# First rows of cumulated logarithms: scanned in the operand's partitions instead of sent there

## The chip, the cores and the metric

One core of a Trainium2 chip runs the whole program. The metric is the device time of one execution in microseconds (us). The engines are PE (TensorE, matrix products), DVE (VectorE), ACT (ScalarE) and POOL (GpSimd); SP is the queue from which all DMAs are issued. PEld is PE's weight load.

## What is computed

Causal attention with a decay from forget gates, and behind it two feed-forward layers on its output:

```python
scores = scale * q @ k.T                       # batch 4, heads 8, sequence 576, head size 64
log_f  = np.log(np.clip(f, 1e-4, 1.0))         # f: one gate per (batch, head, position)
cum    = np.cumsum(log_f, axis=-1)
scores = np.where(causal, -1e9, scores + cum[:, :, :, None] - cum[:, :, None, :])
attn   = softmax(scores) @ v
x = relu(x @ w_in) ** 2 @ w_out                # 2304 tokens, 512 -> 2048 -> 512
x = g(x @ w2_in) @ w2_out                      # g: 0 below -1, (h + 1)**2 / 4, h above 1
```

## The kernel before

**Attention of the first 256 positions** runs in groups of four heads of one batch. A group's operand, the tile `QK` (two buffers, used in turn), holds for each head 256 columns of k and 256 columns of q: rows 0 to 63 are the head's data, and the rows below carry the decay, since a product over 128 rows adds `cum` as two more rows. K's row 64 is `cum` against a q row of -8, and q's row 65 is `cum` against a k row of 8; the rows not used are 8 in k and 0 in q. These fills are memsets at the kernel's start (`clear`, L555). So a group needs its data (L605), its v (L626) and its two rows of `cum` (L618, out of `cumd`, a copy of `cum` in DRAM). Its scores come from L643; L589 on DVE takes the mask and the maximum, L650 on ACT the exponential and its sum, L657 and L658 the reciprocal, L673 to L675 scale on ACT, DVE or POOL, L682 transposes on PE, L570/L573 copy to SBUF, and L695 multiplies with v. In names, s0q, E0q, tr0q, av0q belong to group 0, s1q to group 1, and so on. Groups 0 to 3 make the first block of 512 tokens; group 4 and on belong to the second.

**The start.** `setup` loads the gates f of all 32 (batch, head) pairs into 32 partitions (L485), clips them on DVE (L488), takes the logarithm on ACT (L490) and cumulates it with one scan on DVE (L491). The result goes to DRAM (`cumd`, L503), and for group 0 the two rows of each of its four heads go by two DMAs from `cum` straight into `QK` (`first_rows`, L507). Meanwhile PE multiplies the identity with itself 17 times into a bank that nobody reads (`warm_up`, L542). Q2 and K2, tiles of the second kind of attention (positions 256 on), are filled at the start as well (L517, L518).

**Feed-forward.** The first layer's products (L1042) of step s need the weights `whl` of that step; L1093 to L1095 are the second layer's. Weights arrive as 64-bit words (`raw`, L935, 1 MB a step, the first two steps 512 KB), are decoded on ACT, DVE and POOL (L963 to L984), split into a high and a low half (L1016 to L1019), and stored for later blocks in DRAM (`scr`, L1024). The names whl-2 and whl-1 are the two steps ahead of the plain whl. The first block runs through 32 such steps with new weights; later blocks load them back.

**What sets the order.** The whole program is planned: every operation is put down with its alternatives (which engine, at which assumed cost), a due time and what it depends on; `Schedule.improve` places them on five queues with several weightings (`WEIGHTS`) and emits the best plan found. `QE`, `VE` and `RE` give the earliest time at which the first loads of QK, v and raw may be issued. Each engine runs its queue in order, and SP too: a DMA whose data isn't there holds all DMAs behind it.

Of the kernel before, what the change touches and what calls it, by code (L numbers as in the profile page):

```python
# [16 lines left out]
AF = mybir.ActivationFunctionType  # L17
# [5 lines left out]
P = 128  # L23
# [23 lines left out]
OFF = 512  # L47
QUAD = 4
SPARE = ("E", "g", "E", "o", "E", "r", "E", "g", "E", "o")

SLAV = [0.0, 0.51, 0.75, 0.75, 0.0]
SLQK = [0.0, 0.271, 0.412, 0.414, 0.0]
QE = [0.0, 5.4, 8.66, 11.6]
VE = [5.5, 6.1]
RE = [1.36, 7.73, 16.0]
LW = 29.1
WARM = 17

# [63 lines left out]

WEIGHTS = [{}, *({"DVE": x, "POOL": x * y} for x in (0.4, 0.6, 0.8) for y in (0.0, 0.5, 1.0))]

# [256 lines left out]
def tile_attention_moe_moe(ctx: ExitStack, tc: tile.TileContext, qkv, f, w2, outT):  # L381
# [94 lines left out]
    def setup():  # L476
        sb = new("x", "setup", [P, 2 * NKC * 512], F32)
        fr, lf, cum = (lambda i=i: sb.tile[:H * B, S * i:S * i + S] for i in range(3))
        onesf = lambda: sb.tile[:H * B, 3 * S:4 * S]
        due = -100.0  # L480
        G, V_, A = nc.gpsimd, nc.vector, nc.scalar
        tiny_op.append(sch.op(due - 9, {"POOL": (0.05, lambda: G.memset(tiny, 2.0 ** -30))}))
        oh = sch.op(due - 200, {"POOL": (0.05, lambda: G.memset(warm, 0.5))})
        oh = sch.op(due - 200, {"ACT": (1.5, lambda: A.activation(warm, warm, AF.Ln))}, [oh])
        o1 = sch.op(due, {"SP": (dma_t(73728), lambda: nc.sync.dma_start(out=fr(), in_=f))}, bufs=[sb], early=0.0)  # L485
        o2 = sch.op(due - 5, {"POOL": (0.55, lambda: G.memset(onesf(), 1.0))}, bufs=[sb])
        sch.op(due + 90, {"POOL": (0.05, lambda: G.memset(half, 0.5))})
# [4 lines left out]
            cum(), onesf(), lf(), 0.0, op0=ALU.mult, op1=ALU.add))}, [o4, o2], [sb])  # L492
        sch.op(due, {"ACT": (1.4, lambda: A.activation(warm, warm, AF.Exp))}, [o4])
        hi = lambda: fr().bitcast(F32R)
# [9 lines left out]
            out=cumd, in_=cum()[:, :HEAD]))}, [o5], [sb])  # L504

        def first_rows(row, out, due, deps):
            return sch.op(due, {"SP": (dma_t(4096), lambda: nc.sync.dma_start(  # L507
                out=out(), in_=cum()[row:row + QUAD, :HEAD]))}, [o5, *deps], [sb, QK[0]], early=0.0)

        zs = {}  # L510
        due = -30.0
        for i in range(2):
# [9 lines left out]
        for a, z, md in ((OFF + P - HEAD, OFF + P, -100), (0, OFF + P - HEAD, 60)):  # L522
# [7 lines left out]
            fill=1.0, base=0, channel_multiplier=1))}, [i1])  # L530
        return o7, zs, ms, i2, o8, first_rows

    cum_op, zs, mask_op, id_op, cumd_op, first_rows = setup()
    xb = {0: new("x", "x0")}

# [12 lines left out]
    def clear(i, half):  # L548

        n = QUAD * HEAD  # L550
        rows = lambda a, z: QK[i].tile[a:z, n * half:n * half + n]
        kq = lambda a, z, t: rows(a, z).rearrange("p (c t n) -> p c t n", t=2, n=HEAD)[:, :, t, :]
        due = -98 + 2 * i + half
        eng, m = ("POOL", nc.gpsimd) if i else ("DVE", nc.vector)
        fill = lambda out, x: {eng: (n / 1920 + 0.03, lambda: m.memset(out(), x))}  # L555
        kr = sch.op(due, fill(lambda: kq(D, P, 0), 8.0), [], [QK[i]])
        qr = sch.op(due, fill(lambda: kq(D, P, 1), 0.0), [], [QK[i]])
        return [kr, sch.op(due, fill(lambda: kq(D, D + 1, 1), -8.0), [qr], [QK[i]])]
# [34 lines left out]
    def attention32(g):  # L593
# [13 lines left out]
        row = g.b * H + g.h  # L607
        place = lambda t, c0, c1: reg()[D + t:D + t + 1].rearrange("p (c t n) -> p c t n", t=2, n=HEAD)[:, c0:c1, t, :]
        ready = []
        for i in range(parts):  # L610
            c0, c1 = QUAD * i // parts, QUAD * (i + 1) // parts
            if parts == 2:
                if i == 0:
                    rows = [first_rows(row, lambda t=t: place(t, 0, QUAD), -90, [*cleared[0, 0], *cleared[0, 1]])
                            for t in range(2)]
                ready += [[loads[i], *rows]] * (c1 - c0)
            else:
# [607 lines left out]
```

## Time and profile before

| | us |
|---|---|
| median of 3 runs (lowest, highest) | 947.32 (946.98, 948.59) |
| the profiled execution: its time | 946.77 |
| its span, first to last instruction | 945.0 |
| PE, DVE, ACT, POOL busy in that span | 933.9, 585.9, 638.2, 183.3 |
| PE busy in the first 50 us | 43.79 |

The profile is of one execution; 1.8 us of its time lie outside its span. A timeline row gives start, duration, engine, line, operation, output and inputs, shape and count, and in brackets the engine's idle time before it and what ended that. A row that merges several instructions (x4) has the stretch that they cover. A row of the stages view gives length and busy time of each engine in a stretch, with the number of instructions in brackets, the granted clock of PE (1.00 is the upper level, 2.4 GHz), the share of the DMA engines' time and what they moved. The chain of waits follows the program back from its last instruction.

### The profile page before, as it was taken

To read this page: it belongs to the slowest core of one execution; us is meant where nothing else is said; L and a number is where in the kernel's file an instruction comes from. 1 tells how busy PE (TensorE), PEld (TensorE's weight loads), DVE (VectorE), ACT (ScalarE), POOL (GpSimd) and SP (SyncE) were. 2 spreads that over 40 slices of the span, in tenths; PEclk is the share of its full clock that TensorE was granted. 3 is DMA by queue.
4 is the path that set the end of the run, shared out by engine and by line. 5 is a ranking of instruction groups with operands and counts; after the bars stand their busy time and mean duration, and the time that the engine had idled before them with its cause. 6 is when DMAs were issued, how large, how long until landed. Compare 5 with 4: busy or idle time off the path is not lost.

```text
span 945.0 us, 14242 instructions
## 1 busy us (share of the span) xinstructions
PE 933.9 (99%) x4770; PEld 782.9 (83%) x4770; DVE 585.9 (62%) x1319; ACT 638.2 (68%) x1269; POOL 183.3 (19%) x323
## 2 busy tenths in 40 slices
PE   7999999999999999999999999999999999999998
PEld 5677778877888888888788887888888888889998
DVE  8899999899777659776777668775211132220032
ACT  7988889998887868776777677876523343334444
POOL 3300101324231322432223322321000000002200
PEclk9999999999999999999999999999999999999999
DMA  7799998997999997878789887986655555559993
GB/s 217 230 372 367 333 400 307 369 353 262 342 291 294 276 262 214 278 246 267 228 275 295 224 250 224 291 254 188 250 197 196 204 181 203 195 197 373 366 370 143
DMA packets 126105, 254.72 MB, mean 270 GB/s; under 512 B 89808, under 2 KB 90480, under 8 KB 104080
## 3 DMA queue, kind: packets, MB, share of 16 engines
q1 hardware_dynamic: 126032, 253.81, 80.7%
q8 instruction: 38, 0.62, 0.3%
q14 instruction: 35, 0.29, 0.1%
HBM read 194.35 MB, written 38.45 MB: 246 GB/s over the span
## 4 chain that ended last, share of the span: by engine, by line
PE 92%; DVE 3%; DMA 2%; ACT 1%; issue 1%; POOL 0%; SPq 0%; DVEq 0%; ACTq 0%; POOLq 0%
PE h L1042 40%; PE acc L1093 13%; PE acc L1095 13%; PE acc L1094 13%; PE av L866 4%; PE s L787 2%; PE s L788 2%; DMA PT<-PP 1%; DMA raw-2_209<-in_w_dram 1%; DMA out_dram<-o 1%; DVE PP L841 0%; PE s1q L643 0%; PE s7q L643 0%; PE s4q L643 0%; PE s5q L643 0%
## 5 line engine op out<-in xcount | busy, mean ns | idle before, releaser
L1042 PE MATMUL h<-x,whl 128*128 128x512 f32 (+1 forms) x1896 | 434.7, 372 | 0.4 <-DVE whl L1019 0.3
L1042 PEld LDWEIGHTS h<-x,whl 128*128 128x128 f32 x1896 | 325.0, 188 | 56.4 <-issue 3.0
L1093 PE MATMUL acc<-gh,whl 128*128 128x512 f32 (+1 forms) x640 | 239.2, 374 | 0.7 <-ACT o L570 0.7
L1095 PE MATMUL acc<-gl,whl 128*128 128x512 f32 (+1 forms) x640 | 236.8, 370 | 0.0
L1094 PE MATMUL acc<-gh,whl 128*128 128x512 f32 (+1 forms) x640 | 236.3, 369 | 0.0
L582 DVE TENSOR_TENSOR gl<-g,gh 128x512 fp32r<-128x512 f32 (+1 forms) x122 | 82.7, 678 | 123.3 <-PE acc L1095 82.7
L1095 PEld LDWEIGHTS acc<-gl,whl 128*128 128x128 f32 x640 | 120.5, 188 | 21.2 <-POOL gl L584 0.2
L1093 PEld LDWEIGHTS acc<-gh,whl 128*128 128x128 f32 x640 | 120.6, 188 | 18.8 <-ACT o L570 1.3
L1094 PEld LDWEIGHTS acc<-gh,whl 128*128 128x128 f32 x640 | 120.6, 188 | 15.6
L584 POOL TENSOR_TENSOR gl<-g,gh 128x512 fp32r<-128x512 f32 (+1 forms) x38 | 44.4, 1168 | 341.2 <-PE acc L1095 253.1
L1060 ACT ACTIVATE r<-h 128x512 f32<-128x512 f32 (+1 forms) x80 | 43.9, 549 | 86.8 <-PE h L1042 82.9
L1073 DVE SCALAR_TENSOR_TENSOR g<-r,h 128x512 f32<-128x512 f32 (+1 forms) x80 | 50.5, 631 | 80.5 <-ACT r L1071 80.2
L1069 ACT ACTIVATE r<-h,half 128x512 f32<-128x512 f32 (+1 forms) x80 | 51.1, 639 | 61.0 <-PE h L1042 60.5
L841 DVE SCALAR_TENSOR_TENSOR PP<-E,st,PP 128x512 f16<-128x512 f32 (+2 forms) x128 | 78.2, 645 | 10.4 <-ACT PP L837 9.3
L804 ACT ACTIVATE E<-E,st 64x320 f32<-64x320 f32 (+2 forms) x96 | 63.6, 662 | 26.2 <-DVE st L589 15.8
L589 DVE CUSTOM_DVE_ANT_0 E<-s,mask 128x288 f32<-128x288 f32 (+2 forms) x128 | 61.8, 500 | 24.2 <-PE s L788 15.8
L837 ACT ACTIVATE PP<-E,st 128x512 f16<-128x512 f32 (+2 forms) x128 | 68.6, 591 | 6.3 <-DVE st L811 5.7
L866 PEld LDWEIGHTS av<-pr,vt 128*128 128x128 f32 x288 | 53.5, 188 | 12.0 <-ACT r L1069 0.9
L866 PE MATMUL av<-pr,vt 128*128 128x320 f32 (+2 forms) x288 | 61.5, 285 | 0.5 <-DVE st L589 0.5
L570 ACT ACTIVATE gh<-g 128x512 fp32r<-128x512 f32 (+1 forms) x66 | 38.1, 577 | 30.7 <-DVE g L1073 30.4
L575 POOL TENSOR_SCALAR pr<-PT 128x640 fp32r<-128x640 f16 (+2 forms) x49 | 28.5, 583 | 125.9 <-PE av L866 91.1
L1071 ACT ACTIVATE r<-r 128x512 f32<-128x512 f32 (+1 forms) x80 | 46.9, 587 | 2.0
(250 smaller groups left out, 1112.0 us busy)
## 6 DMA issues: line engine op xcount, KB each, us to landing
whl<-scr SPq DMA_DIRECT2D x112, 1024.0 KB
raw<-in_w_dram SPq DMA_DIRECT2D x28, 1024.0 KB
scr<-whl SPq DMA_DIRECT2D x28, 1024.0 KB
in<-in_qkv_dram SPq DMA_DIRECT2D x32, 608.0 KB
whl<-scr SPq DMA_DIRECT2D x32, 512.0 KB
out_dram<-o SPq DMA_DIRECT2D x16, 256.0 KB
QK<-in_qkv_dram SPq DMA_DIRECT2D x7, 512.0 KB
raw<-in_w_dram SPq DMA_DIRECT2D x6, 512.0 KB
```

What stands on the lines that cost most here:

```text
L582: alts["DVE"] = (dve_t(n), lambda: nc.vector.tensor_sub(out(), a(), b()), True)
L589: return nc.vector.tensor_tensor_reduce(out=out, in0=ps, in1=mask[:m, OFF - q0:OFF - q0 + n], scale=scale, scalar=3e38, op0=ALU.add, op1=A ...
L804: nc.scalar.activation(Ec.tile[:m, :e], Ec.tile[:m, :e], AF.Exp, scale=-1.0, bias=nmx(), accum_out=st.tile[:m, 1, ci:ci + 1])))}, [*tops, ...
L837: nc.scalar.activation(hi, x, AF.Copy, scale=r())
L841: nc.vector.scalar_tensor_tensor(lo, x, r(), hi, op0=ALU.mult, op1=ALU.subtract)
L866: nc.tensor.matmul(av.tile[:, c0:W], vt.tile[:, kc, :, :], pr.tile[:, i, :n], start=(kc == 0 and i == 0), stop=(kc == NK - 1))
L1042: nc.tensor.matmul(ps.tile[:, :n], w.tile[:, 0, wi, kc * P:(kc + 1) * P], src.tile[:, kc, xi, :n], start=(kc == 0 and i == 0), stop=(kc == ...
L1069: o1 = sch.op(due, {"ACT": (act_t(n, True, 1), lambda: A.activation(r.tile[:, :n], ps(), AF.Relu, scale=0.5, bias=half))}, [o], [psb, r])
L1073: o2 = sch.op(due, {"DVE": (dve_t(n), lambda: v.scalar_tensor_tensor(g.tile[:, :n], r.tile[:, :n], 1.0, ps(), op0=ALU.min, op1=ALU.max))}, ...
L1093: nc.tensor.matmul(a.tile[:, :n], wh, gh.tile[:, :n], start=(fc == 0), stop=False)
L1094: nc.tensor.matmul(a.tile[:, :n], wl, gh.tile[:, :n], start=False, stop=False)
L1095: nc.tensor.matmul(a.tile[:, :n], wh, gl.tile[:, :n], start=False, stop=(fc == NFC - 1))
```

## The change

The first two heads of group 0 no longer get their rows by DMA. A new DMA broadcasts their gates, 256 positions each, to partitions 64 to 96 of the setup tile; they are clipped and their logarithm is taken there, and four scans of 256 elements write `cum` into K's row and q's row of each of the two heads, each scan within its own partition. For that q's row moves from partition 65 to 96. The other two heads of the group still get theirs by DMA, now two heads long. The warm-up has 12 products instead of 17. Half of group 0's fills move from DVE to POOL; Q2 and K2 may be filled later; the earliest times of some first loads are put later, and the planner tries three weightings, others than before, instead of seven.

```diff
-QE = [0.0, 5.4, 8.66, 11.6]
-VE = [5.5, 6.1]
-RE = [1.36, 7.73, 16.0]
-WARM = 17
+DIRECT = 2
+ROWS = (64, 96)
+QE = [0.0, 7.0, 8.66, 11.6]
+VE = [6.5, 7.6]
+RE = [2.4, 7.73, 16.0]
+WARM = 12
-WEIGHTS = [{}, *({"DVE": x, "POOL": x * y} for x in (0.4, 0.6, 0.8) for y in (0.0, 0.5, 1.0))]
+WEIGHTS = [{"DVE": x, "POOL": 0.0} for x in (0.6, 0.8, 1.0)]
...
+        b1 = sch.op(due - 2, {"SP": (dma_t(67584), lambda: nc.sync.dma_start(
+            out=first().rearrange("p (c n) -> p c n", n=HEAD),
+            in_=f[:DIRECT, :HEAD].partition_broadcast(ROWS[1] + 1 - ROWS[0])))}, [], [sb], early=0.0)
+        b2 = sch.op(due - 2, {"DVE": (0.37, lambda: V_.tensor_scalar(
+            first(), first(), 1e-4, 1.0, op0=ALU.max, op1=ALU.min))}, [b1], [sb])
+        b3 = sch.op(due - 2, {"ACT": (0.52, lambda: A.activation(first(), first(), AF.Ln))}, [b2, oh], [sb])
...
+        def first_row(head, t, out, deps):
+            return sch.op((-101, -98.2)[head], {"DVE": (0.68, lambda: V_.tensor_tensor_scan(
+                out(), onesf(ROWS[t], ROWS[t] + 1, HEAD), first(ROWS[t], ROWS[t] + 1, head, 1), 0.0,
+                op0=ALU.mult, op1=ALU.add))}, [b3, o2, *deps], [sb, QK[0]])
...
-                out=out(), in_=cum()[row:row + QUAD, :HEAD]))}, [o5, *deps], [sb, QK[0]], early=0.0)
+                out=out(), in_=cum()[row:row + QUAD - DIRECT, :HEAD]))}, [o5, *deps], [sb, QK[0]], early=0.0)
-        due = -30.0
+        due = 30.0
...
-        eng, m = ("POOL", nc.gpsimd) if i else ("DVE", nc.vector)
+        eng, m = ("POOL", nc.gpsimd) if i + half else ("DVE", nc.vector)
```

On DVE, from the kernel's start. QK_180 is group 0's operand, K_0 and K_1 are K2's two buffers, wf-2 the first weights, and L589 the first maximum. Before:

```order
L555 MEMSET QK_180 64x2x256 x3
L488 TENSOR_SCALAR setup<-setup 32x576
L555 MEMSET QK_180 64x2x256
L491 SCALAR_TENSOR_TENSOR setup<-setup 32x576
L518 MEMSET K_0_141 64x576
L518 MEMSET K_1_142 64x576
L978 TENSOR_SCALAR wf-2_238<-wf-2_238 128x512
L980 TENSOR_SCALAR wf-2_238<-wf-2_238 128x512
L983 ISA wf-2_238<-wf-2_238,low_243 128x1024
L589 ISA E0q_256,st0q_268<-s0q_255,mask 128x128
```

Now, where L604 is the first maximum, L517 the new scans and L501 the scan of all heads:

```order
L570 MEMSET QK_180 64x2x256 x2
L570 MEMSET QK_180 1x2x256
L533 MEMSET Q_0_139 64x320
L492 TENSOR_SCALAR setup<-setup 33x512
L498 TENSOR_SCALAR setup<-setup 32x576
L517 SCALAR_TENSOR_TENSOR QK_180<-setup 1x256 x2
L501 SCALAR_TENSOR_TENSOR setup<-setup 32x576
L517 SCALAR_TENSOR_TENSOR QK_180<-setup 1x256 x2
L604 ISA E0q_233,st0q_241<-s0q_232,mask 128x128
```

Fills and the decoding of the first weights have gone from in front of the first maximum, and four scans stand there, two of them in front of the scan of all heads.

On SP, the loads up to group 2. QK_218 is group 1's operand. Before:

```order
L485 DMA setup<-in_f_dram 32x576
L605 DMA QK_180<-in_qkv_dram 64x1024
L935 DMA raw-2_209<-in_w_dram 128x512
L503 DMA cumd<-setup 32x256
L507 DMA QK_180<-setup 1x4x256 x2
L605 DMA QK_218<-in_qkv_dram 64x2048
L626 DMA vt0q<-in_qkv_dram 128x512
L935 DMA raw-1_250<-in_w_dram 128x512
L618 DMA QK_218<-cumd 1x4x256 x2
```

Now, where QK_225 is group 1's operand:

```order
L489 DMA setup<-in_f_dram 33x2x256
L495 DMA setup<-in_f_dram 32x576
L620 DMA QK_180<-in_qkv_dram 64x1024 x2
L953 DMA raw-2_212<-in_w_dram 128x512
L513 DMA cumd<-setup 32x256
L522 DMA QK_180<-setup 1x2x256 x2
L620 DMA QK_225<-in_qkv_dram 64x2048
L644 DMA vt0q<-in_qkv_dram 128x512
L636 DMA QK_225<-cumd 1x4x256 x2
L953 DMA raw-1_270<-in_w_dram 128x512
```

The broadcast stands first, both halves of group 0's data stand ahead of the first weights, and group 1's rows ahead of the second weights.

On SP, a little later, the load of group 3 (QK_218, now QK_225) and the first two full megabytes of weights. Before:

```order
L626 DMA vt2q<-in_qkv_dram 128x512
L935 DMA raw_359<-in_w_dram 128x1024
L605 DMA QK_218<-in_qkv_dram 64x2048
L618 DMA QK_218<-cumd 1x4x256 x2
L935 DMA raw_412<-in_w_dram 128x1024
```

Now:

```order
L644 DMA vt2q<-in_qkv_dram 128x512
L953 DMA raw_364<-in_w_dram 128x1024
L953 DMA raw_373<-in_w_dram 128x1024
L620 DMA QK_225<-in_qkv_dram 64x2048
L636 DMA QK_225<-cumd 1x4x256 x2
```

Both megabytes of weights now go ahead of group 3.

## Rows read from the trace of the kernel before

**Rows 1.** Stages: length, busy us (instructions) per engine, clock, DMA share, GB/s.

```profile
core 0: us, PE busy (x) PEld busy (x) DVE busy (x) ACT busy (x) POOL busy (x), PEclk, DMA share, GB/s
0.00:47.05 47.05, 40.84 (x252) 29.96 (x252) 38.87 (x151) 38.72 (x118) 17.58 (x41) 1.00 0.77 225
47.05:105.00 57.95, 57.95 (x269) 45.27 (x269) 57.02 (x91) 51.22 (x83) 3.35 (x2) 1.00 0.98 375
```

**Rows 2.** Timeline of PE, the first 17 us, and group 3's first products.

```profile
1.39 5.41 PE L542 MATMUL warm<-ident 128*128 128x128 f32 x34 [1.39 <-POOL tiny L482]
9.21 2.86 PE L643 MATMUL s0q<-QK 128*128 128x128 f32 x16 [2.40 <-DMA QK<-setup]
12.98 1.41 PE L682 MATMUL tr0q<-ident,E0q 128*128 128x128 f32 x6 [0.91 <-ACT E0q L673]
15.95 0.89 PE L643 MATMUL s1q<-QK 128*128 128x128 f32 x4
...
28.83 1.48 PE L643 MATMUL s3q<-QK 128*128 128x128 f32 x8
```

**Rows 3.** Timeline of DVE, the first 12 us.

```profile
0.91 2.10 DVE L555 MEMSET QK<- 64x512 f32 x4 [0.91 <-PEq L1207]
3.04 0.45 DVE L488 TENSOR_SCALAR setup<-setup 32x576 f32<-32x576 f32 x1
4.82 1.35 DVE L491 TENSOR_TENSOR_SCAN setup<-setup 32x576 f32<-32x576 f32 x1
6.23 2.36 DVE L518 MEMSET K<- 64x576 f32 x4
9.79 0.69 DVE L983 CUSTOM_DVE_ANT_0 wf-2_238<-wf-2_238,low 128x1024 uint16<-128x1024 uint16 x1 [0.45 <-ACT low L967]
10.40 0.28 DVE L589 CUSTOM_DVE_ANT_0 E0q<-s0q,mask 128x128 f32<-128x128 f32 x1
```

**Rows 4.** Timeline of ACT, the logarithm.

```profile
3.52 0.68 ACT L490 ACTIVATE setup<-setup 32x576 f32<-32x576 f32 x1 [1.30 <-DVE setup L488]
```

**Rows 5.** Timeline of SP, DMA issues.

```profile
0.74 0.41 SPq L485 DMA_DIRECT2D setup<-in_f_dram  x1
...
6.19 0.34 SPq L503 DMA_DIRECT2D cumd<-setup  x1
6.57 1.40 SPq L507 DMA_DIRECT2D QK<-setup  x2
8.02 0.53 SPq L605 DMA_DIRECT2D QK<-in_qkv_dram  x1
...
19.86 0.52 SPq L605 DMA_DIRECT2D QK<-in_qkv_dram  x1
```

**Rows 6.** Stages again: the DMA queue, empty and then full.

```profile
8.00:9.00 1.00, 0.00 (x0) 0.00 (x0) 0.91 (x3) 1.00 (x2) 0.47 (x2) 1.00 0.02 5
9.20:37.00 27.80, 25.72 (x168) 18.08 (x168) 22.81 (x114) 24.52 (x91) 7.42 (x16) 1.00 0.94 276
```

**Rows 7.** Waits up to 47.05 us: who waited for whom, us, times, longest.

```profile
DVE E3q L589 <- PE s3q L643: 1.4, 2, 1.1
DVE E1q L589 <- PE s1q L643: 1.4, 3, 0.7
```

**Rows 8.** Chain of waits, around the first weights of a full step.

```profile
45.87 1.14 DVE whl L1019
...
47.05 2.56 PE h L1042 x10
...
52.45 2.78 PE h L1042 x12
```

**Rows 9.** Timeline of DVE: the split of the next step's weights.

```profile
50.81 1.22 DVE L1019 SCALAR_TENSOR_TENSOR whl<-wf,whl 128x1024 fp32r<-128x1024 f32 x1
```

**Rows 10.** Stages of the warm-up alone, its first and its last part.

```profile
1.39:4.11 2.72, 2.72 (x12) 2.72 (x13) 0.20 (x1) 0.00 (x0) 1.00 0.54 152
4.29:6.53 2.24, 2.24 (x22) 2.24 (x21) 0.20 (x1) 0.00 (x0) 1.00 1.01 245
```

More of the change, by code (lines that the diff above doesn't have):

```diff
@@ L478, in setup @@
         fr, lf, cum = (lambda i=i: sb.tile[:H * B, S * i:S * i + S] for i in range(3))
-        onesf = lambda: sb.tile[:H * B, 3 * S:4 * S]
+        onesf = lambda a=0, z=H * B, n=S: sb.tile[a:z, 3 * S:3 * S + n]
+        first = lambda a=ROWS[0], z=ROWS[1] + 1, c=0, m=DIRECT: sb.tile[a:z, 4 * S + HEAD * c:4 * S + HEAD * (c + m)]
         due = -100.0
@@ L484, in setup @@
         oh = sch.op(due - 200, {"ACT": (1.5, lambda: A.activation(warm, warm, AF.Ln))}, [oh])
+        b1 = sch.op(due - 2, {"SP": (dma_t(67584), lambda: nc.sync.dma_start(
[4 more added lines that the diff above has]
+        b3 = sch.op(due - 2, {"ACT": (0.52, lambda: A.activation(first(), first(), AF.Ln))}, [b2, oh], [sb])
         o1 = sch.op(due, {"SP": (dma_t(73728), lambda: nc.sync.dma_start(out=fr(), in_=f))}, bufs=[sb], early=0.0)
-        o2 = sch.op(due - 5, {"POOL": (0.55, lambda: G.memset(onesf(), 1.0))}, bufs=[sb])
+        o2 = sch.op(due - 5, {"POOL": (0.55, lambda: G.memset(onesf(0, P), 1.0))}, bufs=[sb])
         sch.op(due + 90, {"POOL": (0.05, lambda: G.memset(half, 0.5))})
@@ L492, in setup @@
             cum(), onesf(), lf(), 0.0, op0=ALU.mult, op1=ALU.add))}, [o4, o2], [sb])
-        sch.op(due, {"ACT": (1.4, lambda: A.activation(warm, warm, AF.Exp))}, [o4])
+        sch.op(due, {"ACT": (1.4, lambda: A.activation(warm, warm, AF.Exp))}, [o4, b3])
         hi = lambda: fr().bitcast(F32R)
@@ L504, in setup @@
             out=cumd, in_=cum()[:, :HEAD]))}, [o5], [sb])
+        def first_row(head, t, out, deps):
+            return sch.op((-101, -98.2)[head], {"DVE": (0.68, lambda: V_.tensor_tensor_scan(
+                out(), onesf(ROWS[t], ROWS[t] + 1, HEAD), first(ROWS[t], ROWS[t] + 1, head, 1), 0.0,
+                op0=ALU.mult, op1=ALU.add))}, [b3, o2, *deps], [sb, QK[0]])
         def first_rows(row, out, due, deps):
-            return sch.op(due, {"SP": (dma_t(4096), lambda: nc.sync.dma_start(
-                out=out(), in_=cum()[row:row + QUAD, :HEAD]))}, [o5, *deps], [sb, QK[0]], early=0.0)
+            return sch.op(due, {"SP": (dma_t(2048), lambda: nc.sync.dma_start(
+                out=out(), in_=cum()[row:row + QUAD - DIRECT, :HEAD]))}, [o5, *deps], [sb, QK[0]], early=0.0)
         zs = {}
-        due = -30.0
+        due = 30.0
         for i in range(2):
@@ L530, in setup @@
             fill=1.0, base=0, channel_multiplier=1))}, [i1])
-        return o7, zs, ms, i2, o8, first_rows
-    cum_op, zs, mask_op, id_op, cumd_op, first_rows = setup()
+        return o7, zs, ms, i2, o8, first_row, first_rows
+    cum_op, zs, mask_op, id_op, cumd_op, first_row, first_rows = setup()
     xb = {0: new("x", "x0")}
@@ L607, in attention32 @@
         row = g.b * H + g.h
-        place = lambda t, c0, c1: reg()[D + t:D + t + 1].rearrange("p (c t n) -> p c t n", t=2, n=HEAD)[:, c0:c1, t, :]
+        place = lambda t, c0, c1: reg()[ROWS[t]:ROWS[t] + 1].rearrange("p (c t n) -> p c t n", t=2, n=HEAD)[:, c0:c1, t, :]
         ready = []
@@ L612, in attention32 @@
             if parts == 2:
-                if i == 0:
-                    rows = [first_rows(row, lambda t=t: place(t, 0, QUAD), -90, [*cleared[0, 0], *cleared[0, 1]])
+                for c in range(c0, min(c1, DIRECT)):
+                    ready.append([loads[i], *(first_row(
+                        c, t, lambda c=c, t=t: place(t, c, c + 1)[:, 0, :], cleared[0, i]) for t in range(2))])
+                if c1 > DIRECT:
+                    rows = [first_rows(row + DIRECT, lambda t=t: place(t, DIRECT, QUAD), -90, cleared[0, i])
                             for t in range(2)]
-                ready += [[loads[i], *rows]] * (c1 - c0)
+                    ready += [[loads[i], *rows]] * (c1 - DIRECT)
             else:
```

## The prediction

> **What bounds the kernel now.** I read the stages first. From 47 to 105 us PE is busy 57.95 of 57.95 us at a granted clock of 1.00 [rows 1], and the products there follow each other every 0.23 us (2.78 us for twelve) [rows 8], which is their own length; over the whole span PE is busy 933.9 of 945.0 us. So behind 47 us the kernel is PE's work, and a change at the start is worth what it moves the point at which this dense stretch begins. In the 47.05 us before it, PE is busy only 40.84 [rows 1], and even that includes 5.41 us of warm-up.
>
> Second, PE's timeline. The warm-up ends at 6.80, and PE then waits 2.40 us for the rows of `cum`, a DMA, until 9.21 [rows 2]. Transposes of group 0 start at 12.98, group 1's products at 15.95, group 3's at 28.83 [rows 2]. Third, who is next. In the same 47.05 us DVE is busy 38.87 and ACT 38.72 [rows 1]. The chain of waits runs, right ahead of the dense stretch, not through attention but through DVE: the split of the first full step's weights, 45.87 to 47.01, and PE's products behind it [rows 8]. The next step's split ends at 52.03, and its products start at 52.45 [rows 8, 9]. So DVE's whole queue of the start is nearly as late as PE. Fourth, the DMA queue: it is all but empty at 8 to 9 us (a share of 0.02) and full from 9.2 to 37 us (0.94, 276 GB/s) [rows 6], because SP waits for the scan before it can issue `cumd` and everything behind it [rows 5].
>
> **The rows of the first two heads.** Now: the load of f is issued at 0.74 [rows 5], the clip starts at 3.04, right behind DVE's memsets [rows 3], so the data was there by then. The logarithm takes 0.68 [rows 4], the scan of 576 elements 1.35 and ends at 6.17 [rows 3]; its two DMAs are issued from 6.57 [rows 5], and the first product runs at 9.21, 3.04 us behind the scan's end.
>
> After: the broadcast has f's place in SP's queue, so 3.0 us again. Its clip has 512 elements instead of 576: 0.45 x 512/576 = 0.40, to 3.4. Its logarithm 0.60, to about 4.1 (f's own clip runs meanwhile, its logarithm to 4.8). A scan of 256 elements is 1.35 x 256/576 = 0.60, if the time is in the elements; if most of it is fixed, up to 1.35. I take 0.60, the kind being the same, and keep 1.35 for the range (four of them: 3 us). Two scans end at 5.4, the scan of all heads at 6.75, the other two at 8.0. The warm-up loses ten of 34 passes, at 0.10 us in its last part (22 in 2.24) [rows 10], so it ends near 5.7 and hides behind the scans; nothing is won by it. Head 0's products can run by about 6.2 (the load of its data now has 0.07 MB more ahead of it; it landed somewhere before 9.2), head 1's at 8.1. DVE's first maximum goes from 10.40 [rows 3] to 8.0, since the fills and the decoding of the first weights have gone from in front of it: **2.4 us earlier**. Heads 2 and 3 wait as before for DMAs behind the scan of all heads, whose end moves from 6.17 to 6.75: 6.75 + 3.04 = 9.8, and four products each, half of 2.86 us, end at 11.2. The first transposes stand behind them in PE's queue: 11.3 instead of 12.98, **1.7 us earlier**.
>
> **A load over 33 partitions.** The f load lands within 2.3 us of its issue over 32 partitions [rows 3, 5]; the trace has no load over 33. The Trainium skill, DMA: Bandwidth & Descriptors, section Why a DMA increments its semaphore by 16 and not by 1, says that a DMA of this kind is spread over the largest number of DMA engines, up to 16, that divides the slowest dimension of both sides; 33 partitions would get 11 engines, with 6.1 KB each instead of f's 4.6. By that, as an estimate from this page, the load would take up to a third longer, 0.8 us, and the sum below would be 946.5 instead of 945.7. No run here shows it yet.
>
> **What the DMA queue gives back.** `cumd`, the two row DMAs and group 1's load go out behind a scan that ends 0.6 later, so group 1's load at 8.6 instead of 8.02 [rows 5], and the queue, empty until then, starts that much later. In it group 1's rows now stand ahead of the second weights, 0.52 MB, 1.9 us at 276 GB/s [rows 6]: net 1.3 us earlier, so group 1's products at 14.6 to 15.0 instead of 15.95. Group 3's load loses: a further 1.05 MB of weights stands ahead of it, 3.8 us, and 0.6 from the start. It was issued at 19.86 [rows 5], needs at least 1.9 us, and was used at 28.83, so it landed between 21.8 and 28.8; now between 26.2 and 33.2. By bytes (group 1 to 3's loads at 0.52 MB each, three v at 0.26, the two weights 1.57: 3.9 MB from 9.2 us on) it was 23.4, now 27.8. I take 27.8, which is just in time.
>
> **What DVE gives back.** Taking DVE's rows of both orders up to that split of the first full step, with the durations of before, the sum grows by 1.3 us: scans +2.4, clip +0.4, fills -2.7 (three of QK, three of K2, one of Q2 added), copies out of PSUM that ACT made before +1.7, scalings by the reciprocal +1.2, work on `cum` for later that now comes behind -1.0, decoding -0.7. It was 38.87 busy with 8.2 idle [rows 1]; now 40.2. So the split comes at 40.2 plus DVE's idle time. Of the idle time 1.8 lies before the first maximum in both. The other 6.4 is mostly waiting for products of the next group (1.4 each before groups 1 and 3 [rows 7], which are the longest) and short handovers. If DVE comes to lag rather than lead, the waits for PE go, the handovers stay: I take half, 3.4, as nearest to what is left without these waits. 40.2 + 1.8 + 3.4 = 45.4 instead of 47.0: **1.6 us earlier**. That is also within the 1.7 that PE has at its transposes, and in the next steps it just holds: the split behind has 0.4 us to spare [rows 8, 9]. ACT's sum up to its first work on feed-forward grows by 2.0 (the second logarithm 0.6, nine small scalings instead of three, a split); it idles 8.3 [rows 1] and isn't in the chain there.
>
> The WARM, QE, VE and RE edits and the fewer weightings cost nothing by themselves: they only choose the order, and what of it moves is counted above. Q2 and K2's fills go to POOL, busy 17.58 of 47.05 [rows 1]; if POOL were late, the second kind of attention would wait, tens of us later.
>
> **The sum.** The profiled execution took 946.77 (span 945.0 and 1.8 around it): 946.77 - 1.6 = 945.2. The median of the runs is 0.55 above that execution, so **945.7**. About 0.2% (1.9 us) is what a measurement of this kernel can tell from no change, so this counts as the same.
>
> **Rivals.**
> 1. *The gain stays whole.* DVE's idle time shrinks to handovers alone (2.2 us): 40.2 + 1.8 + 2.2 = 44.2, 2.8 earlier, held to what the first maximum gives, 2.4, to 2.8. For it: PE's queue is full from 16 us on with few waits in it, so it would shift as a block. Against: the split of the next steps. 944.7.
> 2. *Weights and queue take it all.* DVE's idle time falls only by what its work grows (1.3), or group 3's data lands 1.5 us later than by bytes; 947.3.
> 3. *Slower: DVE.* The place is the split of the first full step and the two behind it. If DVE idles as long as before (8.2), because its queue now meets waits for ACT's exponentials and for group 3's data where it had decoding to do, the split comes at 48.4 instead of 47.0, and nothing behind it makes that up, as PE is dense. It decides from an idle time of 6.9 us up. Price 1.3 at 8.2, twice that with group 3 late: 948.6.
> 4. *The clock.* PE held 1.00 through its wait of 2.40 us [rows 1, 2], so shorter, more scattered waits speak for the upper level. In the warm-up the first 12 passes took 0.23 each and the last 22 0.10, with a granted clock shown as 1.00 in both stretches [rows 10]; half the rate is what the lower level (1.2 GHz of 2.4) gives. If PE fell to the lower level between 5.7 and 11, group 0's products and transposes (2.86 and 1.41 us) would take twice as long, +4.3 - 1.6: 950.0. The Trainium skill, TensorE: Matmul & The Clock Gate, Part 1, says that the level is set by how busy the array has been and falls when it idles; by that, with head 0's and head 1's products alone in front of 9.8 us, 950.0 is what it would give, and the row through 2.40 us speaks against it.
>
> **How the numbers follow.** Chances: forecast, 944.9 to 946.7 by an idle time of 2.6 to 4.4, 0.45; rival 1, 0.22; rival 2, 0.16; rival 3, 0.14; rival 4, 0.03. The slower scan (3 us more on DVE's queue, largely in front of the first maximum) lies in rivals 2 and 3. Faster by more than 0.2% means below 945.4: rival 1 and less than a third of the forecast's stretch, 0.35. Slower means above 949.2: rival 4 and a third of rival 3, 0.08. The rest, 0.57, is the same. A range of 943.8 to 948.8 leaves out the top of rival 3, rival 4 and the far end of rival 1.
>
> **What would show it.** Right: first maximum of group 0 on DVE near 8.0, first transposes near 11.3, group 1's products at 14.6 to 15, group 3's near 28, the split of the first full step ending near 45.4 and PE dense behind it at the same pace. Wrong: scans much above 0.6; a broadcast landing after 3.8; DVE idle above 6.9 us before that split; PE waiting for the splits of the next steps; a gap in front of group 3; a granted clock below 1.00; or a changed loss in the later blocks, which this sum leaves as they are.

## The result

| | before | changed |
|---|---|---|
| median of 6 runs, us (lowest, highest) | 947.31 (946.98, 948.85) | 953.18 (950.93, 953.68) |
| ratio to before, 95% interval | | 1.0056 (1.0045 to 1.0067) |
| the profiled execution: time, span, us | 946.77, 945.0 | 953.68, 951.9 |

The changed kernel is slower by 5.9 us, 0.6%. The prediction was 945.7, in a range up to 948.8, so it missed the time and the side. What follows takes the 6.9 us between the two profiled executions apart.

**Where the time went.** First the stages again, of the changed kernel (columns as in [rows 1]); then the chain of waits at the second full step, which stood at 52.45 in [rows 8].

```profile
0.00:47.05 47.05, 40.03 (x232) 30.06 (x233) 41.97 (x152) 38.10 (x114) 13.92 (x35) 0.96 0.74 223
47.05:105.00 57.95, 57.95 (x277) 46.30 (x276) 55.82 (x94) 53.62 (x97) 7.79 (x5) 1.00 0.95 360
```

```profile
54.20 2.72 PE h L1060 x12
```

DVE did 41.97 us of work instead of 38.87, and the granted clock is no longer 1.00. The step's twelve products run 1.75 us later. The other 5.1 of the 6.9 us come behind. The list of PE's waits from 100 to 310 us shows four of half a microsecond or more in the changed kernel; the same list of the kernel before is empty.

```profile
PE h L1060 <- DVE whl L1037: 1.1, 1, 1.1
PE s L805 <- DVE st L604: 1.0, 1, 1.0
PE av L884 <- ACT pr L585: 0.9, 1, 0.9
PE s7q L661 <- DVE st7q L604: 0.5, 1, 0.5
```

**The start, against the forecast.** PE's timeline of the changed kernel, the counterpart of [rows 2]:

```profile
1.40 5.49 PE L557 MATMUL warm<-ident 128*128 128x128 f32 x24 [1.40 <-POOL ident L543]
6.68 1.25 PE L661 MATMUL s0q<-QK 128*128 128x128 f32 x4
...
9.91 1.55 PE L661 MATMUL s0q<-QK 128*128 128x128 f32 x8 [0.47 <-DMA QK<-setup]
11.30 0.49 PE L700 MATMUL tr0q<-ident,E0q 128*128 128x128 f32 x3
...
14.44 0.90 PE L700 MATMUL tr0q<-ident,E0q 128*128 128x128 f32 x3 [1.88 <-DVE E0q L692]
...
16.75 2.07 PE L661 MATMUL s1q<-QK 128*128 128x128 f32 x8
...
22.50 0.63 PE L700 MATMUL tr1q<-ident,E1q 128*128 128x128 f32 x4 [1.17 <-DVE E1q L692]
...
30.83 0.66 PE L700 MATMUL tr2q<-ident,E2q 128*128 128x128 f32 x4 [0.74 <-DVE E2q L692]
...
33.37 1.48 PE L661 MATMUL s3q<-QK 128*128 128x128 f32 x8
```

The one wait of 2.40 us for the rows is gone. In its place stand waits of 0.47 for the rows of heads 2 and 3, and of 1.88, 1.17 and 0.74 us for DVE, which scales by the reciprocal (L692). DVE's timeline tells why (the counterpart of [rows 3], with the split of the first full step last):

```profile
4.27 1.38 DVE L517 TENSOR_TENSOR_SCAN QK<-setup 1x256 f32<-1x256 f32 x2
...
8.49 0.29 DVE L604 CUSTOM_DVE_ANT_0 E0q<-s0q,mask 128x128 f32<-128x128 f32 x1
...
12.28 0.96 DVE L992 TENSOR_SCALAR low<-raw-2_212 128x512 uint16<-128x512 uint16 x1
13.13 0.48 DVE L675 TENSOR_SCALAR st0q<-st0q 128x2 f32<-128x2 f32 x1
...
14.12 0.27 DVE L692 TENSOR_SCALAR E0q<-E0q,st0q 128x128 f32<-128x128 f32 x1
...
45.89 1.22 DVE L1037 SCALAR_TENSOR_TENSOR whl<-wf,whl 128x1024 fp32r<-128x1024 f32 x1
```

The scans take 0.69 each, and the first maximum comes at 8.49, 1.9 us earlier than before. But ahead of head 2's scaling stands decoding (L992), and it and the small L675 take about twice and three times as long as elsewhere, because POOL fills Q2 and the mask's second part at 12 to 14 us, beside them (the run without these fills, new_start_17_mended, shows it).

Behind that wait the clock falls. Stages around it:

```profile
9.20:14.30 5.10, 2.66 (x16) 1.82 (x14) 4.72 (x23) 4.77 (x18) 2.43 (x6) 1.00 0.77 199
14.40:17.80 3.40, 3.36 (x15) 2.23 (x16) 2.15 (x6) 2.12 (x8) 0.61 (x2) 0.50 1.10 297
17.80:37.00 19.20, 17.05 (x111) 12.29 (x109) 17.36 (x75) 16.40 (x57) 2.91 (x5) 1.00 0.96 293
```

PE was busy 2.66 of 5.10 us, and then 3.4 us stand at a granted clock of 0.50, the lower level (1.2 GHz): half of 3.4, 1.7 us, is the most that it can cost in this execution. What of it reaches the second step shows in after_17_warm below, which has the same order with five more warm-up products and a granted clock of 1.00 from 7 to 47 us. Its chain of waits:

```profile
47.52 2.75 PE h L1060 x12
...
52.98 2.72 PE h L1060 x12
```

There the step begins at 52.98. By these two profiles the low stage makes 1.2 of the 1.75 us, and 0.5 are left without it.

### The profile page after: what moved, and what is told of

Read it like the earlier page. It is cut to its first block, busy times and chain, and to the rows that moved or that the text cites. A ratio compares the mean times of both kernels' runs of the same rounds, so it can differ in the third digit from the quotient of the medians.

```text
span 951.9 us, 14257 instructions
## 1 busy us (share of the span) xinstructions
PE 936.4 (98%) x4760; PEld 784.3 (82%) x4760; DVE 596.8 (63%) x1323; ACT 632.0 (66%) x1263; POOL 187.4 (20%) x331
## 4 chain that ended last, share of the span: by engine, by line
PE 88%; DVE 8%; DMA 1%; issue 1%; ACT 1%; POOL 0%; SPq 0%; DVEq 0%; ACTq 0%; POOLq 0%
PE h L1060 39%; PE acc L1111 13%; PE acc L1113 13%; PE acc L1112 13%; PE av L884 4%; PE s L805 2%; PE s L806 2%; DVE whl L1037 2%; DVE low L992 1%; DMA PT<-PP 1%; DVE wf L996 1%; DMA in<-in_qkv_dram 0%; DVE wf L998 0%; DVE wf L1001 0%; DVE gl L597 0%
## 5 line engine op out<-in xcount | busy, mean ns | idle before, releaser
L599 POOL TENSOR_TENSOR gl<-g,gh 128x512 fp32r<-128x512 f32 (+1 forms) x40 | 48.6, 1216 | 297.6 <-PE acc L1113 214.9
L604 DVE CUSTOM_DVE_ANT_0 E<-s,mask 128x288 f32<-128x288 f32 (+2 forms) x128 | 62.1, 501 | 27.6 <-PE s L806 21.3
L590 POOL TENSOR_SCALAR pr<-PT 128x640 fp32r<-128x640 f16 (+2 forms) x55 | 34.3, 628 | 129.8 <-PE av L884 86.3
```

What stands on the lines that cost most here:

```text
L604: return nc.vector.tensor_tensor_reduce(out=out, in0=ps, in1=mask[:m, OFF - q0:OFF - q0 + n], scale=scale, scalar=3e38, op0=ALU.add, op1=A ...
```

## The experiments

The planner was the disturbing factor: any change at the start re-plans all that lies behind. So most kernels here don't plan. Engine and place of each operation come from a table, which was joined from the plans of both kernels at a cut (56 us of the planner's time, where PE's dense stretch has begun); the operations in front of it are those of one start, the others those of one rest. Such a plan has a seam at the cut, which neither of the two plans had, and it may cost something by itself.

```diff
-WEIGHTS = [...]
+PLAN = "..."
...
     def improve(self, pools, rounds):
+        raw, n = zlib.decompress(base64.b85decode(PLAN)), len(self.ops)
+        for i, o in enumerate(self.ops):
+            o.eng, o.start = ENG[raw[i]], float(int.from_bytes(raw[n + 2 * i:n + 2 * i + 2], "big"))
```

| run | start, warm-up products | rest | median, us | ratio to before, interval |
|---|---|---|---|---|
| old_start_new_rest | before, 17 | changed | 951.93 | 1.0052 (1.0040 to 1.0064) |
| new_start_old_rest | changed, 12 | before | 950.16 | 1.0040 (1.0027 to 1.0053) |
| after_17_warm | changed, 17 | changed | 952.37 | 1.0055 (1.0043 to 1.0067) |
| before_12_warm | before, 12 | before | 949.42 | 1.0024 (1.0016 to 1.0033) |
| before_12_late | before, 12, later | before | 948.58 | 1.0017 (1.0008 to 1.0027) |
| new_start_no_scans | changed, no scans, 12 | before | 952.38 | 1.0051 (1.0039 to 1.0063) |
| new_start_17 | changed, 17 | before | 950.35 | 1.0035 (1.0022 to 1.0048) |
| new_start_17_filled | the same, wait filled | before | 949.26 | 1.0022 (1.0012 to 1.0032) |
| new_start_17_mended | changed, mended, 17 | before | 948.80 | 1.0011 (1.0002 to 1.0020) |
| new_start_17_mended_act | the same, copies on ACT | before | 949.04 | 1.0016 (1.0005 to 1.0027) |
| new_start_44_mended | mended, 17 | before, from 44 us | 949.07 | 1.0018 (1.0009 to 1.0027) |
| new_start_44_mended_filled | the same, wait filled | before, from 44 us | 948.31 | 1.0009 (0.9997 to 1.0020) |
| old_start_other_rest_a | before, 17 | other plan of before | 950.40 | 1.0023 (1.0008 to 1.0038) |
| old_start_other_rest_b | before, 17 | other plan of before | 952.77 | 1.0053 (1.0041 to 1.0065) |

Each median is of 5 to 12 executions. The kernel before, measured beside them, had a median of 947.18 for the first four runs but before_12_late; 947.13 for before_12_late, new_start_no_scans, new_start_17 and new_start_17_mended; 947.56 for new_start_17_filled, new_start_17_mended_act and the two other plans; and 947.14 for the two joined at 44 us.

### Start and rest apart

> The changed kernel, but every operation that the planner of the kernel before starts behind 56 us keeps the engine and the place in its queue that it has before; only what starts earlier stands in the changed order. Order theory: of the 6.9 us by which the changed execution is longer, 1.9 are there at the start of the dense stretch (47 us) and 5.0 come between 100 and 310 us from the other order there, so this kernel takes 948 to 949.5 us and PE has no wait of 0.5 us or more between 100 and 310 us. Start theory: the late stalls are consequences of a late DVE and a late DMA queue at the start, whatever the order behind; 952 to 954, with the stalls still there.

> The kernel before, but every operation that the planner of the changed kernel starts behind 56 us stands on the engine and at the place in its queue that it has in the changed kernel; the start is that of before. Order theory: 947.3 plus 5.0, so 951.5 to 953, with PE's waits of about 1 us near 220, 287 and 290 us. Start theory: 947 to 948, without them.

The rest alone costs 4.75 us, as the order theory has it, with the waits that it names. PE's waits from 100 to 310 us in old_start_new_rest:

```profile
PE av L866 <- ACT pr L570: 1.1, 1, 1.1
PE h L1042 <- DVE whl L1019: 1.1, 1, 1.1
PE s L787 <- DVE st L589: 1.0, 1, 1.0
PE acc L1093 <- ACT o L570: 0.9, 1, 0.9
PE s7q L643 <- DVE st7q L589: 0.7, 1, 0.7
```

The start theory falls: the start of before doesn't remove them. Nor is it the join: the longest wait from 47 to 100 us is 0.3 here. With the changed start and the old rest they are gone (the longest there is 0.4), but the time is 3.0 us above before, more than expected; the rest of that is taken up below. Both parts together give 5.9, not 7.7. A wait may absorb some of a lateness that reaches it, and the join in new_start_old_rest may cost something that the changed kernel doesn't pay (a wait of 0.9 at 76.8 us, taken up under Mending the start); no run tells the two apart.

How the changed order makes such a wait is seen at 278 to 292 us of the changed kernel, in its chain of waits and, below, in SP's issues:

```profile
278.33 0.44 SPq L866
278.86 4.66 DMA in<-in_qkv_dram
283.61 0.69 ACT K L585
```

```profile
258.37 9.08 SPq L866 DMA_TRANSPOSE PT<-PP  x3
...
272.78 5.99 SPq L866 DMA_TRANSPOSE PT<-PP  x2
278.86 0.53 SPq L748 DMA_DIRECT2D in<-in_qkv_dram  x1
```

The load of a head's q, k and v (`in`) stands on SP behind two transposes that hold the queue for 5.99 us; K and the scores behind that load come late, and PE waits.

### Is the order of before special?

> The kernel before, start and all, but what its planner starts behind 56 us stands in the order of another of its own plans: the same weighting (DVE 0.8, POOL 0), two rounds of improvement later, which the planner rates 0.04 us longer. Order theory: what an order is worth behind 56 us is not known to the planner within some us, since small waits that it doesn't see come and go; this kernel differs from before by 1 us or more, most likely slower, 948 to 952. Rival: equal plans take equal times, 946.8 to 947.6.

> As old_start_other_rest_a, with the rest from a plan of another weighting (DVE 0.6, POOL 0, fifth round) which the planner rates 0.18 us longer. Order theory: differs from before by 1 us or more, 948 to 952, and from old_start_other_rest_a as well. Rival: 946.8 to 947.8.

Two other plans of the kernel before, rated 0.04 and 0.18 us longer by its planner, took 2.8 and 5.2 us longer on the chip. Part of the 2.8 is the clock: six of the nine executions of rest a have a mean granted clock of 0.998, and the low stage of its profile (0.50 at 15.4 to 18.6 us) lies in the start. In rest b the order theory holds, and the order of before is the best of the three plans of this kernel that were measured: PE's two longest waits behind 47 us, at 200 to 400 us and so far from the cut, are longer than any such wait in before, where the one for `whl` is 0.3 and the one for `pr` isn't found. A third, of 1.0 us for group 4's transposes, lies nearer to the cut.

```profile
PE av L866 <- DVE pr L573: 2.3, 1, 2.3
PE h L1042 <- DVE whl L1019: 1.7, 2, 1.4
```

The edit of WEIGHTS did nothing by itself: both kernels are emitted from the same weighting (DVE 0.8, POOL 0), which stands in both lists. What re-drew the plan is the start.

### The warm-up and the clock

```diff
-        sch.op(-90, {"PE": (0.43 * WARM, lambda: mms(WARM))}, [id_op], [ps])
+        sch.op(-90, {"PE": (0.43 * WARM, lambda: mms(17))}, [id_op], [ps])
```

> The changed kernel with its order kept as it is and 17 warm-up products emitted instead of 12. Clock theory: the granted clock of 0.55 to 0.59 at 14 to 18 us comes from the shorter warm-up; with 17 it stays at 1.00 in 9 to 20 us, and the 1.3 to 1.8 us of that stretch are won: 951.4 to 952. Rival: the dip has to do with PE's idle 1.88 us in front of group 0's later transposes and not with the warm-up; it stays in some executions and the time is that of the changed kernel, 953.2, or up to 1 us more where a longer warm-up at the slow rate delays head 0.

> The kernel of run new_start_old_rest (changed start, order of before behind 56 us) with 17 warm-up products instead of 12. Clock theory: the shorter warm-up costs at the clock, as before_12_warm gave 2.2 us more than before; so 948 to 949, with the mean granted clock at 1.000 in most executions. Rival: the warm-up is hidden in the changed start, as it ends by 8.5 us; 950.2 as without, with the same share of executions at a mean clock below 1.000.

> The kernel before with its order kept as it is and 12 warm-up products emitted instead of 17. Clock theory: a dip of the clock or a later rise costs 1 to 2 us, 948.3 to 949.3, with a granted clock below 1.00 in 9 to 18 us. Rival: nothing, 947.3, since the products wait for the rows of cum at 9.2 us in any case.

With the changed start, 17 products instead of 12 change nothing that these runs tell (952.37 against 953.18, 950.35 against 950.16). The kernel before loses 2.2 us with 12. Its profile shows no low clock in that; PE's waits behind 47 us are longer instead (2.3 us in two for the copies of a block's results, `acc` behind ACT's `o`, against 0.7 before). Yet nine of its eleven executions have a mean granted clock of 0.998 or less, and of the 17 of before beside it only one, so much of the 2.2 us can be the clock, which the profiled execution (0.999) doesn't show. For before_12_late, POOL made a second identity ahead of its fills, and the products used that:

```diff
-                nc.tensor.matmul(ps.tile[:, :P], ident, ident, start=True, stop=True)
+                nc.tensor.matmul(ps.tile[:, :P], late, late, start=True, stop=True)
```

> The kernel before with its order and 12 warm-up products that multiply a second identity, which POOL makes 0.5 us of work later, so that they run from about 3.2 us on and end at about 8.3 instead of 6.5, right ahead of the first product at 9.2. Clock theory: PE's idle time in front of the first product is what costs the 2.2 us of before_12_warm; 947.0 to 947.6, mean clock 1.000 in most executions. Rival: the number of products or something else of the program's form costs them; 949 to 949.6.

948.58 lies between the two expectations and its interval overlaps that of before_12_warm, so neither is shown. Its twelve executions fall in two halves by the clock: six at 0.998 or less with a median of 950.2, six at 0.999 or more with 947.9. In the profiled one the low stage isn't in the start at all but at 474 us, right behind a wait of PE for `acc`:

```profile
472.65 0.50 PE L1093 MATMUL acc<-gh,whl 128*128 128x512 f32 x1 [2.06 <-ACT o L570]
```

```profile
474.00:477.40 3.40, 3.40 (x11) 2.82 (x10) 1.31 (x3) 2.49 (x7) 0.33 (x2) 0.50 1.07 272
```

So what the old start loses with twelve products is in large part lower clock, as far as the mean clocks tell. Why twelve products bring it on there stays open.

The wait itself, filled with products whose result is written over:

```diff
-            got = [sch.op(t0 + 3, {"PE": (0.11, lambda tr=tr, Eb=Eb, to=to, at=at: nc.tensor.transpose(
+            got = [sch.op(t0 + 3, {"PE": (0.11, lambda tr=tr, Eb=Eb, to=to, at=at: [nc.tensor.matmul(tr.tile[:, :P], ident, ident, start=True, stop=True) for _ in range(8 * (g.i == 0 and c == 2 and to == 0))] and 0 or nc.tensor.transpose(
```

> The kernel of run new_start_17 with eight products of the identity with itself, whose result is written over at once, put on PE in front of group 0's third transposes, where it waits 1.9 us for DVE's scaling. Clock theory: the granted clock of 0.50 at 14.7 to 18.2 us there (1.7 us lost) comes from this wait; with PE busy in it, 1.00 throughout 9 to 20 us and 948.4 to 949.0 instead of 950.35. Rival: the dip comes from somewhere else or is given back behind; 950 to 950.7.

The first stage here is new_start_17, the second new_start_17_filled:

```profile
14.80:18.10 3.30, 3.30 (x15) 2.18 (x14) 1.79 (x5) 1.65 (x6) 0.61 (x2) 0.50 1.04 268
```

```profile
14.40:17.80 3.40, 3.31 (x26) 2.48 (x24) 3.24 (x12) 2.73 (x10) 0.59 (x2) 1.00 1.00 272
```

With PE kept busy the low stage is gone, and the median is 1.1 us less, just above the expected range; the two intervals overlap. The mean granted clock was 0.997 or 0.998 in all five executions of new_start_17, and 1.000 in nine of the twelve with the wait filled.

### What the scans bring

> The kernel of run new_start_old_rest (12 products) without the broadcast, its clip and logarithm and the four scans: all four heads of group 0 get their rows by DMA as before, and everything else keeps its engine and place. Gain theory: the scans bring the first maximum forward by 1 us or more, and that is worth something: 950.5 to 951.5. Rival: the four scans (2.8 us) and the clip on DVE's queue cost what they bring, since heads 2 and 3 and all of DVE's work behind come later by them: 949 to 950.2, not slower than with the scans.

Without the scans 952.38, above both expectations; with them 950.16. The intervals overlap, and what the scans are worth isn't shown apart from the clock. The first maximum comes at 9.73 without them instead of 8.49. But all five executions without scans have a mean granted clock of 0.996 to 0.998 (the profile has two stages of over 3 us at 0.50, from 9.4 and from 16.3 us on, the first of them amid group 0's products), and the three with scans at 0.997 or 0.998 took 950.20, 952.63 and 952.66, hardly less; at 1.000 the others took 949.5 to 950.1. Whether the earlier rows spare the clock by themselves or the two differ by chance stays open.

### Mending the start

On DVE decoding and split go behind the scaling (here at 13 us; likewise behind the scalings of groups 1 and 2), and on POOL the fills of Q2, K2 and the mask's second part go to a later time. The order on DVE:

```diff
-L992 TENSOR_SCALAR low<-raw-2 128x512
 L675 TENSOR_SCALAR st0q<-st0q 128x2
 L676 RECIPROCAL st0q<-st0q 128x2
+L692 TENSOR_SCALAR E0q<-E0q,st0q 128x128
+L992 TENSOR_SCALAR low<-raw-2 128x512
 L996 TENSOR_SCALAR wf-2<-wf-2 128x512
-L692 TENSOR_SCALAR E0q<-E0q,st0q 128x128
```

> The kernel of run new_start_17 with a handful of operations moved: on DVE the decoding and the split of the first weights stand behind the scalings of groups 0 to 2 for which PE waits (1.9, 1.2 and 0.7 us), and the fills of Q2, K2 and the mask's second part, which POOL does at 12 to 14 us beside them, are done behind 150 us. DVE theory: these three waits are what ate the gain of the earlier rows; without them PE's waits shrink by 2 us or more and the dense stretch begins 1 to 2 us earlier than in new_start_17, the time is 1 to 2 us less. Rival: behind them stands the same split of the first full step's weights on DVE, whose sum of work is unchanged, so the dense stretch begins where it did and the time is the same within 0.5 us.

1.55 us less than new_start_17, and the intervals are just apart; among executions with a mean clock of 0.998 or less it is 948.86 against 950.35. So the DVE theory holds for the start, though the edit moves DVE's operations and POOL's fills at once and doesn't tell which of the two brought it. The waits for DVE go from 1.9, 1.2 and 0.7 to 1.0, 0.7 and none. With POOL quiet, L992 and L675 are back at their length (timeline of DVE):

```profile
12.85 0.17 DVE L675 TENSOR_SCALAR st0q<-st0q 128x2 f32<-128x2 f32 x1 [0.49 <-ACT E0q L668]
13.26 0.29 DVE L692 TENSOR_SCALAR E0q<-E0q,st0q 128x128 f32<-128x128 f32 x1
13.46 0.46 DVE L992 TENSOR_SCALAR low<-raw-2_217 128x512 uint16<-128x512 uint16 x1
```

Still 1.7 us above before. PE's dense stretch now leads by 0.9 us, and at 75 us PE waits as long in one wait:

```profile
75.63 0.87 PE L700 MATMUL tr4q<-ident,E4q 128*128 128x128 f32 x6 [0.93 <-ACT E4q L691]
```

It looks like the lead that is lost again, and the next runs took it for that. But the same wait stands where there is no lead to lose: in new_start_17, whose dense stretch is later than that of before, and in new_start_no_scans, later still and without the scans (one row of each):

```profile
78.32 0.88 PE L700 MATMUL tr4q<-ident,E4q 128*128 128x128 f32 x6 [0.93 <-ACT E4q L691]
```

```profile
79.72 0.88 PE L682 MATMUL tr4q<-ident,E4q 128*128 128x128 f32 x6 [0.93 <-ACT E4q L673]
```

Every kernel here with the changed start that was joined at 56 us has it, 0.92 to 0.94 us long; neither before nor the changed kernel as planned has it. So it goes with the join of the changed start to the rest of before. In new_start_17_mended the chain of waits leads back from it through DVE to 58 us, where DVE's L1001 takes 2.32 us instead of 1.23 beside a subtraction that the changed plan had given to POOL (the rows are in the last section).

> The kernel of run new_start_17_mended with four copies out of PSUM in groups 1 to 3 moved from DVE to ACT (1.7 us of DVE's work). DVE theory: behind an earlier start of the dense stretch DVE is the next to be late (PE waits 0.9 us at 75 us for scalings of group 4, behind DVE's maxima); with less on DVE that wait falls below 0.5 us and the time by 0.5 to 1.2 us, to 947.6 to 948.3. Rival: ACT is as late there (53.8 us of its scaling in the same stretch), so the wait stays and the time is the same, 948.8.

> The kernel of run new_start_17_mended, but with the order of before from 44 us of the planner's time on instead of 56, so that the scalings of group 4 and the subtraction at 57.8 us go back from POOL to DVE and ACT. Sharing theory: POOL's work beside DVE made DVE 1 us late at 58 us, and by that PE at 75 us; without it PE's wait at 75 us is below 0.5 us, at least 0.5 us of the 0.9 us of lead stay, and the time is 0.6 to 1.2 us less than that of new_start_17_mended: 947.5 to 948.2. Rival: DVE is full from 36 us on anyway and its sum of work at the start has grown, so its lateness just shows elsewhere; 948.5 to 949.2.

> The kernel of run new_start_44_mended with five products of the identity with itself on PE in front of group 0's third transposes, where it waits 1.0 us. Clock theory: 0.3 to 0.8 us less in the median than without, as fewer executions fall to the lower level, 947.0 to 947.6. Rival: a wait of 1.0 us costs no clock; the same within 0.3 us.

Four copies moved to ACT leave the wait at 0.9: that theory falls. With POOL's work away, L1001 is back at 1.23 and the wait at 75 us is gone, so the sharing theory is right about that wait. It is wrong about the time, 949.07: another wait of 0.91 for group 4's scalings stands at 54 us, again just behind this kernel's own cut, where the chain of waits runs through ACT. The rival, that the queues of DVE and ACT are late by themselves, fits the time; that each cut behind the changed start costs some 0.9 us by itself fits it as well, and no run tells them apart. The stages 36 to 47.05 and 47.05 to 76 us, first of before, then of new_start_17_mended:

```profile
36.00:47.05 11.05, 10.71 (x60) 7.46 (x58) 9.47 (x27) 9.98 (x24) 3.48 (x3) 1.00 0.50 162
47.05:76.00 28.95, 28.95 (x135) 22.92 (x136) 28.69 (x44) 26.09 (x44) 1.54 (x1) 1.00 0.98 377
```

```profile
36.00:47.05 11.05, 10.73 (x65) 8.30 (x65) 10.98 (x29) 10.96 (x24) 0.00 (x0) 1.00 0.59 222
47.05:76.00 28.95, 28.02 (x130) 21.98 (x129) 28.48 (x46) 26.03 (x47) 5.09 (x4) 1.00 0.99 353
```

From 47 to 76 us DVE is busy 28.69 of 28.95 us before the change as well: it is nearly as full as PE. A lead of PE may be worth little there unless DVE leads too, but this is argued and not shown: the lead was only ever tried in front of a seam. Filling the last wait (1.1 us, five products) takes 0.8 us off, the most that the clock theory gave it, though the time itself stays above its 947.6: the mean granted clock is 0.998 in nine of eleven executions without and in one of eleven with. The intervals overlap. At 948.31 it is the best of the changed starts and no different from before by its interval; no kernel here beats before.

## Why the prediction was wrong

- *Load, clip, logarithm, rows, first transposes: right.* The broadcast was there when DVE came to its clip at 3.04; rows of heads 2 and 3 at 9.91 (9.8 forecast), first transposes at 11.30 (11.3). The scans took 0.69, not 0.60, and the first maximum came at 8.49, not 8.0. The 0.8 us more that the prediction estimated for the load over 33 partitions, by the Trainium skill, DMA: Bandwidth & Descriptors, section Why a DMA increments its semaphore by 16 and not by 1, don't show: issued at 0.74, its data was clipped from 3.04 on.
- *The warm-up ends near 5.7: wrong,* 6.89. Its 24 passes took 0.23 us each; in before they go from 0.23 to 0.10 at 4.3. So by the rate of the passes (the granted clock reads 1.00 in both) the clock had not risen by the warm-up's end. By the Trainium skill, TensorE: Matmul & The Clock Gate, Part 1, what decides the level runs freely and isn't set off by a kernel's start; the profiles agree, since the rise came at 4.3 in one and behind 6.9 us in the other with the same work up to then.
- *The path: wrong.* The prediction let the dense stretch move with the end of DVE's split of the first full step. In after_17_warm, at 1.00, that split ended at 45.90, 1.1 us earlier than before, and the products of the second step still came 0.5 us later than in before. PE's twelve products of the first full step follow other work of PE without a gap there: what was late was PE's own queue, which had waited in the start. Up to 47 us PE waits 5.4 us in the changed kernel, against 4.6 before, with the wait ahead of the warm-up left out; 3.8 of the 5.4 are the three waits for scalings, which the prediction didn't have.
- *Group 1's products at 14.6 to 15: wrong,* 16.75. The data was not what was late. Group 0's third transposes stand ahead of them in PE's queue and waited 1.88 us for DVE. The prediction followed DMAs and the first maximum and didn't follow PE's own queue to its next wait. Group 3's products (33.37, not 28) came late by the same queue; PE waits for no DMA ahead of them.
- *DVE's sum: the mis-sized term.* It was to grow by 1.3 us up to the split of the first full step, to 40.2; it grew by 3.1, to 41.97. In the profiled execution its idle time was 5.1, the 5.2 that was assumed, so the split ended at 47.11 and not at 45.4; but part of that idle time came with the low stage. At 1.00, in after_17_warm, the work is the same 42.0 and the idle time 3.9:

```profile
44.68 1.22 DVE L1037 SCALAR_TENSOR_TENSOR whl<-wf,whl 128x1024 fp32r<-128x1024 f32 x1
```

  That end, 45.90, is near the forecast by luck: two errors that cancel. Four instructions beside POOL alone make 2.1 of the work: L992 0.96 for 0.46, L675 0.48 for 0.17, the clip of f 0.74 for 0.45, and a scaling at 29 us, 1.32 for 0.35, beside POOL's decoding; the scans make 0.4 more, and smaller groups gave some back. For L992 and L675 new_start_17_mended shows that POOL is the cause; for the other two (below) it shows only that POOL works beside them. "Q2 and K2's fills go to POOL" was weighed for POOL and not for DVE. The Trainium skill, SBUF — State Buffer, section SBUF: two separate sides, says that DVE and POOL share a pair of ports that one of them holds for a whole instruction; the trace agrees for L992 and L675, with these numbers.

```profile
3.50 0.74 DVE L498 TENSOR_SCALAR setup<-setup 32x576 f32<-32x576 f32 x1
```

```profile
L692 DVE TENSOR_SCALAR E2q<-E2q,st2q x3: 346/353/1322, 29.2 to 31.9; 128x256 f32<-128x256 f32 x2, 128x128 f32<-128x128 f32 x1
```

- *The clock: a rival with 0.03.* The level fell, not between 5.7 and 11 us but at 14.4, behind a wait for DVE that the prediction didn't see, and cost at most 1.7 us in the profiled execution, 1.2 at the second step, and not 4.3.
- *"PE's work behind 47 us": true of PE, but not the whole.* DVE was nearly as full, with the numbers in the rows. Whether that eats a lead isn't shown: the wait of 0.9 at 54 or 75 us goes with the joins.
- *"Later blocks are left as they are": the largest error,* 3.0 us (953.18 against 950.16) to 4.75 (951.93 against 947.18) of the 5.9. The edits of QE, VE, RE and the fills "only choose the order" was taken as a cost of nothing. The order behind 56 us was drawn anew, and plans that the planner holds nearly equal lie up to 5 us apart. It shows in PE's waits for late copies, scores and weights behind 100 us: 3.5 us in the four listed in the result.

In sum: the rows came earlier as planned, the first maximum by 1.9 us, but what that is worth isn't shown apart from the clock. The new start as planned lost it in PE's own queue, through DVE's longer work ahead of the scalings and the lower clock behind the wait, and the new draw of the rest, which the prediction put at nothing, is the largest part of the 5.9.

What stays open: what five warm-up products do in the old start, what the changed start would bring with a rest that was planned for it and drawn as well as that of before, what a join costs, and why the wait for a block's copies (`acc` behind `o`) is 0.3 us in one profile and 2.3 in another under the same order.

## What to carry over

Where a planner orders the whole program, measure an edit with the rest of the order held fixed, and measure a few plans of equal rating before believing any of them; the spread here, 5 us, is more than the edit could win. A plan joined from two has a seam that can cost by itself: look for waits just behind the cut, and compare joined kernels with joined kernels. Before counting a lead of the engine on the critical path as won, follow that engine's own queue to its next wait, and look for a second engine that is as full in the stretch behind. And when work is moved to POOL, price what it does to the DVE instructions beside it, not only POOL's own time.

## Of the hardware, not expected

- POOL's work beside DVE lengthened single DVE instructions by 0.3 to 1.1 us. In new_start_17_mended POOL's subtraction and DVE's combining of the weights:

```profile
57.84 1.78 POOL L599 TENSOR_TENSOR gl<-g,gh 128x512 fp32r<-128x512 f32 x1 [2.89 <-ACT gh L1084]
```

```profile
58.38 2.32 DVE L1001 CUSTOM_DVE_ANT_0 wf<-wf,low 128x2048 uint16<-128x2048 uint16 x1
```

  The same instruction takes 1.23 us at 70 us, without POOL.
- A wait of 1.9 us was followed by the lower clock in some profiles and not in others with the same start: new_start_17 fell to 0.50 behind it, new_start_old_rest and after_17_warm, with the same wait, show 1.00 from 9 to 20 us.
- A scan of 256 elements takes 0.69 us and one of 576 takes 1.35, so by these two points some 2.1 ns an element and 0.16 fixed, an estimate.
